# Splitting GpSimd's elementwise operations into two halves in a fused attention and expert kernel

## The chip, the cores and the metric

The kernel runs on one core of one Trainium2 chip. The metric is the device time of one execution in microseconds, given as the median of several runs. The times before are 1339.83, 1334.39 and 1337.75 us, median 1337.75.

A core has five engines that work side by side, each with an instruction queue of its own: TensorE (PE in the profile; PEld is its weight load), VectorE (DVE), ScalarE (ACT), GpSimd (POOL) and SyncE (SP, here the issuer of almost all transfers). They wait for each other by semaphores.

## The reference

```python
q_lm, k_lm = segment_mean(q), segment_mean(k)      # 576 rows to 32 landmarks
A, Bm, C = sm(q, k_lm), sm(q_lm, k_lm), sm(q_lm, k)
Z = Bm.T / (norm1(Bm) * norminf(Bm) + 1e-6)
for _ in range(6):
    Z = 2 * Z - Z @ Bm @ Z
x = A @ Z @ C @ v                                  # 8 batches, 8 heads, 576 x 64
x = relu(x @ w_in) ** 2 @ w_out                    # 4608 x 512, hidden 2048
e = argmax(x @ w_gate)                             # one of 8 experts for a token
out = gate(x, e) * sigmoid(x @ w_output_gate)[e] * (relu(x @ w1[e]) @ w2[e])   # hidden 1024
```

`sm` is a scaled softmax of a matrix product; everything is float32.

## The kernel before, in words

The work goes by batch (8 of 576 tokens). Three kinds of work share the core:

- **Attention of a batch** (`unit`): sums of segments (`sums`, line 382), scores, three softmaxes, the iterated inverse (`inverse`), all small. `softmax_a` (lines 463 to 478) takes the 128 x 576 scores `aa`: VectorE's maximum (468), GpSimd's subtraction (469), ScalarE's exponential (472), VectorE's sum and reciprocal (474 to 476), GpSimd's product (477), VectorE's transpose (671). Attention's product with the first weight is folded into a matrix `g` for a batch, made from `win` (`g_alone`, `g_steps`).
- **The first feed-forward network of a batch** (`gemm`, `second`): two column halves `c` of 288 tokens, and in each 16 blocks `f` of 128 hidden units. A block is 6 matmuls (line 998), ReLU on ScalarE (1009), two squares (1011 on VectorE or 1013 on ScalarE, and 1014), the low part `gl` on VectorE (1015), then 12 matmuls into four accumulators (1048).
- **The experts** (`experts`): batch by batch, 8 blocks of 128 hidden units, 24 matmuls (line 1238) and 14 more (1274, 1286) a block.

Products are made in a reduced format with two parts for each operand: `split` (line 186) lets ScalarE round a tile to a high part (188), and then GpSimd, or VectorE where `lo_eng` says so, subtracts it from the raw tile to give the low part (191). TensorE then multiplies high by high, high by low and low by high. The low parts on GpSimd are those of `gb` (from `gr`), `ab` (from `ar`), `wi`, three of four `wo`, the activations `xs` (128 x 1152) and the first weights `s` of the experts (128 x 512); the second weights' go to VectorE.

Weights of the first network pass through `convert` (lines 137 to 184), which rebuilds a 32-bit float from two integer words: ScalarE makes `m` and `r` (153, 154), VectorE shifts and joins bits (163, 164), GpSimd adds the two as integers (167). Two kinds of job use it: `w_in`, whose result goes to memory as `win`, and `w_out`, whose result is split into `wo`.

Around 40 to 130 us the conversions and the attention of the first batches run together with the first blocks of `gemm`. Up to about 700 us the attention of later batches runs as side work beside `gemm`: at each `point` a share of a side step (RATES, RATE) is put into the program. From about 700 to 910 us `gemm` runs almost alone; from there on it is the experts. `behind` and `follow` add ordering edges that pace TensorE and ScalarE. The program is laid out by a planner that orders each engine's queue by priority and a timed model of the program (it is told `schedule_with_timeline_sim=True`); within a queue the order is then fixed. SyncE's queue issues the transfers: `win`, `g`, `at`, `x2`, the experts' weights. GpSimd issues 9 small ones.

The expert weights are prepared one block ahead of their use:

```python
            fetch_w(i + 2)
            flush()
            h = hidden(i)
            parts_w(i + 1)
```

Of the kernel before, what the change touches and what calls it, by code (L numbers as in the profile page):

```python
# [9 lines left out]
F32 = mybir.dt.float32  # L10
F32R = mybir.dt.float32r
I32 = mybir.dt.int32
U32 = mybir.dt.uint32
ACTF = mybir.ActivationFunctionType
ALU = mybir.AluOpType
# [68 lines left out]
class Kernel:  # L84
# [42 lines left out]
    def convert(self, jobs):  # L127

        nc, pool = self.nc, self.cv
        W = CONV_W
        pieces = [(j, c) for j in range(len(jobs)) for c in range(0, 512, W)]
        st, to = {}, {}  # L140
        RB = CONV_AHEAD

        def fetch(i):
            j, c = pieces[i]
            raw = pool.tile([128, W, 2], I32, tag="raw", name="raw", bufs=RB)
            nc.sync.dma_start(out=raw, in_=jobs[j][0][:, c:c + W].bitcast(I32).rearrange("p (n t) -> p n t", t=2))
            st[i] = raw

        def scale(i):
            raw = st[i]  # L150
            m = pool.tile([128, W], I32, tag="cm", name="m", bufs=CONV_BUFS)
            r = pool.tile([128, W], I32, tag="cr", name="r", bufs=CONV_BUFS)
            first = nc.scalar.activation(out=m.bitcast(F32), in_=raw[:, :, 1].bitcast(F32), func=ACTF.Abs, scale=2.0 ** -111)
            nc.scalar.activation(out=r, in_=raw[:, :, 0].bitcast(U32), func=ACTF.Copy, scale=2.0 ** -29)
            if self.last_gb is not None:
                self.follow(first, self.last_gb)
            st[i] = raw, m, r

        def bits(i):
            (j, c), (raw, m, r) = pieces[i], st.pop(i)  # L160
            if c == 0:
                to[j] = jobs[j][1]()
            nc.vector.tensor_scalar(out=m, in0=m, scalar1=3, scalar2=None, op0=ALU.logical_shift_left)
            nc.vector.scalar_tensor_tensor(  # L164
                out=m, in0=raw[:, :, 1], scalar=-0x80000000, in1=m, op0=ALU.bitwise_and, op1=ALU.bitwise_or
            )
            nc.gpsimd.tensor_tensor(out=to[j][:, c:c + W].bitcast(I32), in0=m, in1=r, op=ALU.add)

        n = len(pieces)
        for i in range(min(RB - 1, n)):  # L170
            fetch(i)
        yield STEP
        per = 512 // W
        for i in range(n + 4):
            if i + RB - 1 < n:
                fetch(i + RB - 1)
            if i < n:
                scale(i)
            if 0 <= i - 1 < n:
                bits(i - 1)  # L180
            if i >= 2 and (i - 2) % per == per - 1 and i - 2 < n:
                j = (i - 2) // per
                jobs[j][2](to.pop(j))
            yield STEP

    def split(self, t, raw, lo_eng=None, late=False):

        hi = self.nc.scalar.copy(out=t[:, 0], in_=raw)  # L188
        if late and self.last_h is not None:
            self.follow(hi, self.last_h)  # L190
        (lo_eng or self.nc.gpsimd).tensor_tensor(out=t[:, 1], in0=raw, in1=t[:, 0].bitcast(F32), op=ALU.subtract)  # L191

    def convert_in(self):

# [268 lines left out]
    def softmax_a(self, u, hg):  # L463
        nc = self.nc
        ma = u["ma"][:, :, hg]
        af = u["aa"][:, hg].rearrange("p (n l) -> p n l", l=LM)
        wide = [128, NB, LM]
        nc.vector.tensor_reduce(out=ma[:, 0], in_=af, axis=AX.X, op=ALU.max)
        (nc.vector if u["early"] else nc.gpsimd).tensor_tensor(
            out=af, in0=af, in1=ma[:, 0].unsqueeze(2).to_broadcast(wide), op=ALU.subtract  # L470
        )
        nc.scalar.activation(out=af, in_=af, func=ACTF.Exp, scale=SCALE / SEG)
        yield STEP
        nc.vector.tensor_reduce(out=ma[:, 1], in_=af, axis=AX.X, op=ALU.add)
        nc.vector.tensor_scalar(out=ma[:, 1], in0=ma[:, 1], scalar1=1e-9, scalar2=None, op0=ALU.add)
        nc.vector.reciprocal(out=ma[:, 2], in_=ma[:, 1])
        nc.gpsimd.tensor_tensor(out=af, in0=af, in1=ma[:, 2].unsqueeze(2).to_broadcast(wide), op=ALU.mult)
        yield STEP

    def scores_c(self, u, hg, c):  # L480
# [1017 lines left out]
```

## Time and profile before

| | |
|---|---|
| median of 3 runs | 1337.75 us (1334.39 to 1339.83) |
| profiled execution | 1340.34 us, span 1338.5 us |
| TensorE busy | 1275.7 us, 95% |
| VectorE busy | 781.5 us, 58% |
| ScalarE busy | 633.6 us, 47% |
| GpSimd busy | 384.5 us, 29%, 311 instructions |
| mean granted TensorE clock | 0.977 of full speed |

The span is the time from the first to the last instruction on the chip. Busy time of GpSimd and VectorE counts an instruction from its start in the record to its end; when it starts and can't go on, the wait is inside. Busy shares are means over stages with different limits. The chain that ended last is followed back from the last instruction, at each step to what released it; it tells whose time set the end.

### The profile page before, as it was taken

The page shows a single profiled execution, that of the slowest core. Times are in us where ns is not written, and L with a number is a line of the kernel's source. Part 1 is how long each engine was busy: PE and PEld are TensorE (multiplying, and loading weights), DVE is VectorE, ACT ScalarE, POOL GpSimd, SP SyncE. Part 2 cuts the span into 40 slices and gives each one's busy share as a digit, 9 for nine tenths or more (in the row PEclk, how much of TensorE's full clock was granted, in tenths as well). Part 3 has the DMA queues.
Part 4 walks back from the last instruction along what each step waited for, and adds up shares of the span by engine and source line. Part 5 has one row for each costly group of instructions (what it writes and reads, how often), then busy time and mean ns, then how long its engine had stood idle before and what let it go on. Part 6 is the DMA issues. An engine that isn't in the chain of part 4 may idle for free.

```text
span 1338.5 us, 25101 instructions
## 1 busy us (share of the span) xinstructions
PE 1275.7 (95%) x9458; PEld 1114.2 (83%) x9458; DVE 781.5 (58%) x1743; ACT 633.6 (47%) x1402; POOL 384.5 (29%) x311
## 2 busy tenths in 40 slices
PE   6587999999999999999999999999999999999997
PEld 4276868688788888898989999998888888888886
DVE  7999868768769897687653433454423233233231
ACT  5596454445535557545654344344334334334331
POOL 3566112113013034313622112024323323233120
PEclk7588999999999999999999999999999999999999
DMA  9866283462623247613652112014344354342321
GB/s 324 273 222 192 86 269 85 173 199 89 217 70 112 72 127 211 172 63 95 206 146 67 43 35 67 1 48 146 99 130 139 100 156 120 109 150 92 116 93 38
DMA packets 126587, 172.38 MB, mean 129 GB/s; under 512 B 10558, under 2 KB 84062, under 8 KB 126462
## 3 DMA queue, kind: packets, MB, share of 16 engines
q1 hardware_dynamic: 126030, 170.11, 41.6%
q8 instruction: 76, 1.25, 0.4%
q0 software_dynamic: 288, 0.43, 0.1%
q14 instruction: 49, 0.40, 0.1%
q10 hardware_dynamic: 144, 0.20, 0.0%
HBM read 128.19 MB, written 42.51 MB: 128 GB/s over the span
## 4 chain that ended last, share of the span: by engine, by line
PE 74%; DVE 11%; DMA 7%; ACT 3%; issue 2%; POOL 1%; SPq 1%; POOLq 0%; DVEq 0%; ACTq 0%
PE acc L1048 24%; PE hp L1238 15%; PE y L1274 13%; PE hp L998 11%; PE bank L346 6%; PE y L1286 2%; DMA raw<-in_moe_w_in_dram 2%; DVE sums L382 2%; DVE gl L1015 2%; DMA g<-gs 2%; DVE g L1011 1%; PE pl L1075 1%; DVE m L164 1%; DMA w<-win 1%; DMA t<-in_q_dram 1%
## 5 line engine op out<-in xcount | busy, mean ns | idle before, releaser
L1048 PE MATMUL acc<-gh,wo 128*128 128x288 f32 x2048 | 459.2, 300 | 1.6 <-POOL wo L191 0.7
L1048 PEld LDWEIGHTS acc<-gh,wo 128*128 128x128 f32 x2048 | 344.1, 190 | 27.1 <-issue 18.2
L1048 PE MATMUL acc<-gl,wo 128*128 128x288 f32 x1024 | 290.3, 301 | 10.2 <-DVE gl L1015 9.7
L998 PE MATMUL hp<-ab,gb 128*128 128x288 f32 x1536 | 254.8, 301 | 0.9 <-ACT r L1009 0.5
L998 PEld LDWEIGHTS hp<-ab,gb 128*128 128x128 f32 x1536 | 217.7, 189 | 19.6 <-issue 6.9
L1011 DVE TENSOR_TENSOR g<-r 128x288 f32<-128x288 f32 x239 | 130.3, 546 | 162.5 <-ACT r L1009 161.7
L1009 ACT ACTIVATE r<-hp 128x288 f32<-128x288 f32 x256 | 105.8, 413 | 245.1 <-PE hp L998 240.6
L1238 PEld LDWEIGHTS hp<-xs,s 128*128 128x128 f32 x1536 | 210.7, 188 | 9.0 <-issue 0.9
L1238 PE MATMUL hp<-xs,s 128*128 128x288 f32 x1536 | 215.5, 295 | 0.0
L1048 PEld LDWEIGHTS acc<-gl,wo 128*128 128x128 f32 x1024 | 194.6, 190 | 22.8 <-DVE gl L1015 17.5
L1274 PE MATMUL y<-s,h 128*128 128x512 f32 x768 | 190.3, 395 | 0.0
L1274 PEld LDWEIGHTS y<-s,h 128*128 128x128 f32 x768 | 141.0, 188 | 29.4
L1015 DVE TENSOR_TENSOR gl<-g,gh 128x288 fp32r<-128x288 f32 x256 | 143.2, 560 | 26.8 <-ACT gh L1014 8.9
L191 POOL TENSOR_TENSOR s<-r,s 128x512 fp32r<-128x512 f32 x64 | 83.1, 1299 | 245.6 <-ACT s L188 245.6
L191 DVE TENSOR_TENSOR s<-r,s 128x512 fp32r<-128x512 f32 x64 | 53.1, 830 | 154.4 <-ACT s L188 154.4
L191 POOL TENSOR_TENSOR gb<-gr,gb 128x512 fp32r<-128x512 f32 x56 | 74.5, 1331 | 226.6 <-ACT gb L188 143.6
L188 ACT CAST s<-r 128x512 fp32r<-128x512 f32 x128 | 78.2, 616 | 118.8 <-PE y L1286 92.6
L1247 DVE SCALAR_TENSOR_TENSOR h<-hp,h 128x64 fp32r<-128x64 f32 (+2 forms) x192 | 62.6, 354 | 109.5 <-ACT h L1244 109.5
L1014 ACT ACTIVATE gh<-r 128x288 fp32r<-128x288 f32 x256 | 114.4, 447 | 6.4
L1244 ACT ACTIVATE h<-hp 128x288 fp32r<-128x288 f32 x128 | 52.6, 411 | 132.1 <-PE hp L1238 118.2
L382 DVE TENSOR_REDUCE sums<-t 128x32 f32<-128x576 f32 x64 | 71.2, 1165 | 9.3 <-DMA t<-in_q_dram 5.8
L191 POOL TENSOR_TENSOR xs<-xr,xs 128x1152 fp32r<-128x1152 f32 x16 | 45.7, 2860 | 68.3 <-ACT xs L188 63.2
(195 smaller groups left out, 1350.8 us busy)
## 6 DMA issues: line engine op xcount, KB each, us to landing
r<-in_moe_w_dram SPq DMA_DIRECT2D x128, 256.0 KB
w<-win SPq DMA_DIRECT2D x80, 256.0 KB
gr<-g SPq DMA_DIRECT2D x56, 256.0 KB
t<-in_k_dram SPq DMA_DIRECT2D x16, 576.0 KB
t<-in_q_dram SPq DMA_DIRECT2D x16, 576.0 KB
v<-in_v_dram SPq DMA_DIRECT2D x48, 192.0 KB
x_d<-x SPq DMA_DIRECT2D x16, 576.0 KB
xr<-x_d SPq DMA_DIRECT2D x16, 576.0 KB
```

Of the source, the lines that this page charges most:

```text
L188: hi = self.nc.scalar.copy(out=t[:, 0], in_=raw)
L191: (lo_eng or self.nc.gpsimd).tensor_tensor(out=t[:, 1], in0=raw, in1=t[:, 0].bitcast(F32), op=ALU.subtract)
L346: self.last_pe = self.nc.tensor.matmul(out, **kw)
L382: self.nc.vector.tensor_reduce(out=s[:, 0, ds], in_=t[:, :, ds].rearrange("p s d -> p d s"), axis=AX.X, op=ALU.add)
L998: mm = nc.tensor.matmul(hp[:, 0:HC], lhsT=g[:, l, hg, fs], rhs=at[:, r, hg, :], start=(i == 0), stop=(i == 5))
L1009: nc.scalar.activation(out=r, in_=hp[:, 0:HC], func=ACTF.Relu, scale=1.0 / 256)
L1011: nc.vector.tensor_tensor(out=g2, in0=r, in1=r, op=ALU.mult)
L1014: nc.scalar.activation(out=gh, in_=r, func=ACTF.Square)
L1015: nc.vector.tensor_tensor(out=gl, in0=g2, in1=gh.bitcast(F32), op=ALU.subtract)
L1048: nc.tensor.matmul(acc[m][:, 0:HC], lhsT=self.wo[f][:, l, ms], rhs=r, start=(f == 0 and i == 0), stop=(f == NFC - 1 and i == 2),)
L1238: nc.tensor.matmul(hp[:, 0:HC], lhsT=s1[:, l, kk, :], rhs=xs[j, c][:, r, kk, :], start=(k == 0), stop=(k == 3 * KD - 1),)
L1274: mm = nc.tensor.matmul(acc[t], lhsT=l, rhs=s2[:, r, :], start=(first and k == 0), stop=(last and k == 2))
```

## The change

Every elementwise operation of GpSimd on data is issued as two instructions of half the columns each: the integer add of `convert`, the low parts of `split` and the two of `softmax_a`. For operands with three axes the halves are taken along the second axis. Operations of VectorE stay whole, and so does GpSimd's copy of the sums (line 385).

```diff
@@ convert
-            nc.gpsimd.tensor_tensor(out=to[j][:, c:c + W].bitcast(I32), in0=m, in1=r, op=ALU.add)
+            self.halves(to[j][:, c:c + W].bitcast(I32), m, r, ALU.add)
@@ split
-        (lo_eng or self.nc.gpsimd).tensor_tensor(out=t[:, 1], in0=raw, in1=t[:, 0].bitcast(F32), op=ALU.subtract)
+        if lo_eng is None:
+            self.halves(t[:, 1], raw, t[:, 0].bitcast(F32), ALU.subtract)
+        else:
+            lo_eng.tensor_tensor(out=t[:, 1], in0=raw, in1=t[:, 0].bitcast(F32), op=ALU.subtract)
+
+    def halves(self, out, in0, in1, op):
+
+        n = out.shape[1]
+        for p in (slice(0, n // 2), slice(n // 2, n)):
+            self.nc.gpsimd.tensor_tensor(out=out[:, p], in0=in0[:, p], in1=in1[:, p], op=op)
@@ softmax_a
-        (nc.vector if u["early"] else nc.gpsimd).tensor_tensor(
-            out=af, in0=af, in1=ma[:, 0].unsqueeze(2).to_broadcast(wide), op=ALU.subtract
-        )
+        most = ma[:, 0].unsqueeze(2).to_broadcast(wide)
+        if u["early"]:
+            nc.vector.tensor_tensor(out=af, in0=af, in1=most, op=ALU.subtract)
+        else:
+            self.halves(af, af, most, ALU.subtract)
...
-        nc.gpsimd.tensor_tensor(out=af, in0=af, in1=ma[:, 2].unsqueeze(2).to_broadcast(wide), op=ALU.mult)
+        self.halves(af, af, ma[:, 2].unsqueeze(2).to_broadcast(wide), ALU.mult)
```

## Rows read from the trace of the kernel before

**Rows 1.** The page: busy time of the engines, and the chain's shares by engine.
```profile
PE 1275.7 (95%) x9458; PEld 1114.2 (83%) x9458; DVE 781.5 (58%) x1743; ACT 633.6 (47%) x1402; POOL 384.5 (29%) x311
...
PE 74%; DVE 11%; DMA 7%; ACT 3%; issue 2%; POOL 1%; SPq 1%; POOLq 0%; DVEq 0%; ACTq 0%
```

**Rows 2.** Busy us by stretch: PE, PEld, DVE, ACT, POOL; clock, DMA share, GB/s.
```profile
40.00:130.00 90.00, 66.59 (x542) 49.70 (x541) 86.78 (x140) 67.77 (x158) 57.80 (x44) 0.81 0.71 223
...
400.00:550.00 150.00, 143.97 (x1263) 127.99 (x1257) 125.36 (x258) 86.60 (x201) 50.74 (x45) 1.00 0.46 140
...
910.00:1339.00 429.00, 418.79 (x2473) 372.23 (x2471) 136.32 (x311) 153.48 (x294) 122.52 (x83) 0.99 0.39 114
```

**Rows 3.** Groups by shape of POOL, count; busy, mean ns; idle before, releaser.
```profile
L191 POOL TENSOR_TENSOR s<-r,s 128x512 fp32r<-128x512 f32 x64 | 83.1, 1299 | 245.6 <-ACT s L188 245.6
...
L191 POOL TENSOR_TENSOR ab<-at,ab 128x576 fp32r<-128x576 f32 x1 | 1.6, 1603 | 0.0
```

**Rows 4.** Timeline of DVE: start us, duration us, what, idle before.
```profile
75.17 0.69 DVE L164 SCALAR_TENSOR_TENSOR m<-raw,m 128x512 int32<-128x512 int32 x1
...
76.52 1.07 DVE L163 TENSOR_SCALAR m<-m 128x512 int32<-128x512 int32 x1 [0.33 <-ACT m L153]
77.63 1.66 DVE L164 SCALAR_TENSOR_TENSOR m<-raw,m 128x512 int32<-128x512 int32 x1
...
740.49 0.46 DVE L1011 TENSOR_TENSOR g<-r 128x288 f32<-128x288 f32 x1 [1.31 <-ACT r L1009]
...
890.74 2.20 DVE L1011 TENSOR_TENSOR g<-r 128x288 f32<-128x288 f32 x1 [1.30 <-ACT r L1009]
893.07 0.46 DVE L1015 TENSOR_TENSOR gl<-g,gh 128x288 fp32r<-128x288 f32 x1
```

**Rows 5.** Groups by shape of DVE.
```profile
L1015 DVE TENSOR_TENSOR gl<-g,gh 128x288 fp32r<-128x288 f32 x256 | 143.2, 560 | 26.8 <-ACT gh L1014 8.9 <-DVE g L1011 0.5 <-DVE bc L587 0.3
L1011 DVE TENSOR_TENSOR g<-r 128x288 f32<-128x288 f32 x239 | 130.3, 546 | 162.5 <-ACT r L1009 161.7
...
L164 DVE SCALAR_TENSOR_TENSOR m<-raw,m 128x512 int32<-128x512 int32 x32 | 32.3, 1010 | 0.6
```

**Rows 6.** Timeline of POOL.
```profile
76.03 1.28 POOL L167 TENSOR_TENSOR w<-m,r 128x512 int32<-128x512 int32 x1 [1.78 <-DVE m L164]
77.27 1.47 POOL L191 TENSOR_TENSOR wo<-w,wo 128x512 fp32r<-128x512 f32 x1
...
889.95 2.67 POOL L191 TENSOR_TENSOR xs<-xr,xs 128x1152 fp32r<-128x1152 f32 x1 [32.31 <-ACT xs L188]
897.74 2.67 POOL L191 TENSOR_TENSOR xs<-xr,xs 128x1152 fp32r<-128x1152 f32 x1 [5.12 <-ACT xs L188]
```

**Rows 7.** The chain in order of time: start us, us, what (some of its pieces).
```profile
49.12 1.50 DVE m L164
...
84.41 1.34 POOL w L167
...
129.04 0.93 DVE dg L647
...
357.48 1.35 DVE gl L1015
...
646.57 1.19 DVE ma L475
...
662.79 1.31 POOL wi L191
...
1009.58 3.17 PE hp L1238 x24
...
1016.02 3.19 PE hp L1238 x24
```

**Rows 8.** PE alone by stretch: us, busy us (instructions), clock, DMA share, GB/s.
```profile
640.00:660.00 20.00, 19.58 (x141) 1.00 0.65 192
...
720.00:740.00 20.00, 20.00 (x154) 1.00 0.23 71
```

## Prediction

> **What bounds the kernel now.** I first read the page's busy shares and the shares of the chain that ended last. TensorE is busy 95% of the span and carries 74% of the chain; VectorE carries 11% and GpSimd 1%, at 29% busy [rows 1]. An engine with so much room can be made less efficient without harm, unless its work stands in someone's way. So the second view is the busy time by stage [rows 2]. From 40 to 130 us VectorE is busy 86.8 of 90 us and TensorE only 66.6: VectorE is the bound there. From 400 to 550 us both are nearly full (125 and 144 of 150). From 910 us to the end TensorE has 418.8 of 429 us and GpSimd's 122.5 us lie wholly beside it.
>
> The third view is the list of instruction groups. The change splits eleven GpSimd groups, from 64 low parts of `s` to the one of `ab` [rows 3]: 258 instructions in all.
>
> The fourth is the timeline, and it shows what GpSimd does to VectorE. Undisturbed, lines 1011 and 1015 take 0.46 us each and line 164 takes 0.69 [rows 4]; their means over the run are 0.546, 0.560 and 1.010 us [rows 5]. The excess is 239 x 0.086 + 256 x 0.10 + 32 x 0.32 = 56 us. Where it comes from is seen at 77.63 us: line 164 lasts 1.66 us [rows 4] while a GpSimd subtraction runs from 77.27 to 78.74 [rows 6]; 78.74 plus the line's own 0.6 is its end, 79.29. VectorE waited until the whole GpSimd instruction was over. At 890.74 us line 1011 lasts 2.20 us beside a GpSimd instruction that runs from 889.95 to 892.62 [rows 4, 6]: the same.
>
> The last view is the chain in order of time: which of these waits set the end. From 40 to 130 us it holds 15 VectorE pieces of 0.87 us or more that are at most 0.69 undisturbed, the first at 49.12, the last at 129.04 [rows 7]: 20.0 us less 6.8 undisturbed, 13.2 us of waiting. From 330 to 700 us there are 12 such, 357.48 to 646.57 [rows 7], 15.9 less 4.2, so 11.7 us. Near 900 us there are two, the first at 890.74 [rows 4], of 1.75 us excess each. That is 28 us of waiting on the chain. GpSimd's own elementwise instructions on it are 13, from 84.41 to 662.79 [rows 7].
>
> **The change part by part.** *Two instructions for one.* Alone, 512 columns take 1.28 us and 1152 take 2.67 [rows 6]: 2.17 ns a column and 0.17 us beside. A half of 512 columns is thus 0.73 us, a pair 1.45 less the 0.04 us by which back-to-back records overlap (76.03 + 1.28 against 77.27) [rows 6]: +0.13 us a pair, 258 x 0.13 = 33 us more of GpSimd. It has 950 us free, and in the last stage each low part is made one step ahead, 6.4 us (1016.02 less 1009.58) [rows 7]: hidden there at 0. If that lead were gone, the 64 low parts of `s` would cost 8 us. On the chain it is 13 x 0.13 = 1.7, say +1.5 us. The wait of ScalarE or VectorE on a low part moves to the second half; that is this same 0.13 us, with nothing else queued behind.
>
> *Halves let VectorE in sooner.* No row shows a split operation, so I bound it. At best each wait on the chain halves: 13.2 to 6.6, 11.7 to 5.9, 3.5 to 1.8, a gain of 14 us. At worst nothing is gained. What decides is the instruction behind the one that waited. At 76.52 us line 163 waits, runs, and line 164 behind it waits again, for the next GpSimd instruction [rows 4, 6]: the two engines take turns. With halves, VectorE's first gets in after 0.73 us, GpSimd's second half then goes, and VectorE's second waits for that. If both VectorE instructions need their turn, the later ends as before. At 890.74: the first half would end at about 891.36, line 1011 at 891.8, the second half at 893.2, line 1015 at 893.65; today that ends at 893.53 [rows 4]. Gain 0, so I take **0 for the third term**. From 40 to 130 us lines 163, 164, 191 and 1015 follow each other closely with VectorE 96% busy, nearest to this case: **-1.5 us** of 0 to -6.6. From 330 to 700 us I count five waiting pieces of line 1015, which often has a transpose or a reduction behind it, five of line 1011, with 1015 following, and two others. Half of the former's 4.5 us is gained, and a tenth of the other 7.2: **-3 us** of 0 to -5.9.
>
> Whether VectorE gets a turn between two halves is the open step. The rows at 76.52 and 77.27 show that line 163 got in between two back-to-back GpSimd instructions: the wait ended as the first ended (77.31), and the second lasted 1.47 rather than 1.28 us [rows 4, 6]. I take it so. The Trainium skill, GPSIMD Engine Reference, section Instruction dispatch, speaks against it: completion of a Pool instruction "does not hold back the next Pool instruction", a core begins the next as soon as its share is done. By that rule the halves would run as one, the gains would be zero and the sum +1.5 us or a little more; no row here shows a pair with nothing at all between.
>
> *Sum:* -1.5 - 3 + 0 + 1.5 = -3 us. The profiled execution took 1340.3 us, 2.6 above the median of 1337.75. So 1337.3 by that execution and **1335 us** by the median: no difference of note, since a measurement of this kernel can tell about 0.5% (6.7 us). When the waits shrink, the next late thing is TensorE's own queue (144 of 150 us busy from 400 us on).
>
> **The rivals.** *Full relief (faster).* Non-waiting VectorE work fills the turns, all waits halve, and the lost time downstream (gl late, matmuls late) returns too: -14 + 1.5, so about 1325. For it: VectorE near its limit in both stretches. Against: the turns at 76.52 and 890.74.
>
> *The halves are not parted (no change).* The port stays taken through both: waits as before, each 0.13 us longer; 29 waits x 0.13 + 1.5 is +5: 1343. The row at 77.27 speaks against it [rows 6]. The section of the Trainium skill named above leads here.
>
> *Late pairs (slower).* Place: the run of GpSimd work on the chain from 636 to 664 us (seven of the 13) and at 309 to 316 (three). Now GpSimd too waits at two starts: VectorE's 0.45 to 0.69 us twice, so a pair can reach 1.41 + 0.55 to 0.69, 2.0 to 2.1 us, in place of 1.3. Price: 13 x 0.75 = 10 us with no relief: 1348. It decides where the mean pair, first start to last end, passes 1.28 + 0.55 = 1.83 us (13 x 0.55 = 7 us) while lines 1011 and 1015 don't fall below their present means. For it: GpSimd instructions follow each other on the chain around 640 us. Against: GpSimd has 1% of the chain in all [rows 1].
>
> *Another order.* The queues' order comes from a planner that times the program; 258 more instructions may reorder all engines. No row shows how its order depends on such lengths. One more disturbed stretch costs little: TensorE starts 141 instructions in 640 to 660 us against 154 in 720 to 740 [rows 8], 13 x 0.13 = 1.7 us in 20. Four to five such would pass 0.5%; it can go either way, 1327 to 1345.
>
> **How the numbers follow.** The forecast has 0.40 (its own range 1330 to 1341); full relief 0.22; unparted halves 0.10; late pairs 0.13; another order 0.15. Faster by over 0.5%: all of full relief, 0.05 of the forecast, 0.06 of another order: 0.33. Slower: all of late pairs, 0.05 of unparted halves, 0.06 of another order and 0.02 of the forecast: 0.26. Same is the rest, 0.41. The range runs from below full relief, 1321, to the late pairs' 1348.
>
> **What would show it.** Right: means of lines 1011 and 1015 near 0.50 us, line 164 near 0.85; pairs of 512 columns at 1.4 to 1.6 us; 569 GpSimd instructions; the stage from 910 us on unchanged in length; the stretch of 40 to 130 us shorter by under 5 us. Wrong: line 1015 unchanged (unparted halves); a pair mean over 1.83 us with more GpSimd on the chain (late pairs); 400 to 550 us shorter by over 5 us (full relief); other neighbours in the queues with a moved stage (another order).

## The result and the profile after

The changed kernel takes 1325.18 us (median; 1323.49 to 1326.16) against 1337.93 before: ratio 0.9903, 95% interval [0.9887, 0.9919], so 12.8 us or 1.0% faster. The forecast was 1335 us.

The page of the changed kernel, busy times and the chain, against [rows 1]:

```profile
PE 1270.4 (96%) x9458; PEld 1110.4 (84%) x9458; DVE 751.2 (57%) x1743; ACT 634.2 (48%) x1402; POOL 439.7 (33%) x569
...
PE 80%; DVE 9%; DMA 4%; ACT 3%; issue 2%; POOL 1%; SPq 0%; POOLq 0%; ACTq 0%; DVEq 0%
```

GpSimd does 258 instructions more and is busy 55 us longer; VectorE, whose instructions are the same 1743, is busy 30 us less. Lines 1011 and 1015 are now 1022 and 1026; helper line 200 issues all halves. Groups by shape of VectorE, against [rows 5], then two of GpSimd:

```profile
L1022 DVE TENSOR_TENSOR g<-r 128x288 f32<-128x288 f32 x239 | 120.5, 505 | 167.8 <-ACT r L1020 166.8
...
L1026 DVE TENSOR_TENSOR gl<-g,gh 128x288 fp32r<-128x288 f32 x256 | 135.7, 531 | 25.7 <-ACT gh L1025 7.9 <-DVE g L1022 0.5
...
L164 DVE SCALAR_TENSOR_TENSOR m<-raw,m 128x512 int32<-128x512 int32 x32 | 28.1, 879 | 0.7
```

```profile
L200 POOL TENSOR_TENSOR s<-r,s 128x256 fp32r<-128x256 f32 x128 | 97.4, 782 | 233.5 <-ACT s L188 233.5
```

The excess of the three VectorE groups over their undisturbed times falls from 56 us to 239 x 0.045 + 256 x 0.071 + 32 x 0.19 = 35 us. A pair of `s` has 97.4 / 64 = 1.52 us of busy time, where one whole operation had 1.30 [rows 3].

The stretches, against [rows 2]:

```profile
40.00:130.00 90.00, 70.97 (x583) 54.16 (x580) 81.91 (x146) 70.34 (x164) 71.39 (x87) 0.82 0.71 230
400.00:550.00 150.00, 147.80 (x1312) 131.85 (x1311) 120.83 (x270) 87.87 (x201) 61.68 (x84) 1.00 0.50 149
```

In the same 150 us TensorE starts 1312 matmuls in place of 1263, and VectorE, with 12 instructions more (270 against 258), is busy 4.5 us less.

How one wait changed is seen in the timeline of GpSimd (first fence) and VectorE (second) at the place that was 890 us before [rows 4, 6]:

```profile
874.03 3.02 POOL L200 TENSOR_TENSOR xs<-xr,xs 128x576 fp32r<-128x576 f32 x2 [32.17 <-ACT xs L188]
```

```profile
874.81 0.95 DVE L1022 TENSOR_TENSOR g<-r 128x288 f32<-128x288 f32 x1 [1.30 <-ACT r L1020]
875.90 1.47 DVE L1026 TENSOR_TENSOR gl<-g,gh 128x288 fp32r<-128x288 f32 x1
```

Line 1022 got in between the halves: it lasts 0.95 us in place of 2.20. GpSimd's pair took 3.02 us instead of 2.67; 0.13 us of that is the estimate for a second start, the rest is the wait of its second half. Then line 1026 waited for that half. From the start of line 1022 to the end of line 1026 it is 2.56 us, and was 2.79: two waiters, hardly any gain. The Trainium skill, GPSIMD Engine Reference, section Instruction dispatch, says that the completion of a GpSimd instruction does not hold back the next one; the row shows that VectorE is let in between two halves all the same.

The order of the queues changed as well, on every engine: the planner placed the program anew. VectorE's sequence of conversions, blocks and attention is another one from its 100th instruction on, which starts at 44.29 us. So two things happened at once, and the first experiments part them.

### The profile page after: what moved, and what is told of

Its sections match the earlier page's. It is cut to its first block, busy times and chain, and to the rows that moved or that the text cites. A ratio compares the mean times of both kernels' runs of the same rounds, so it can differ in the third digit from the quotient of the medians.

```text
span 1321.8 us, 25393 instructions
## 1 busy us (share of the span) xinstructions
PE 1270.4 (96%) x9458; PEld 1110.4 (84%) x9458; DVE 751.2 (57%) x1743; ACT 634.2 (48%) x1402; POOL 439.7 (33%) x569
## 4 chain that ended last, share of the span: by engine, by line
PE 80%; DVE 9%; DMA 4%; ACT 3%; issue 2%; POOL 1%; SPq 0%; POOLq 0%; ACTq 0%; DVEq 0%
PE acc L1059 26%; PE hp L1249 15%; PE y L1285 13%; PE hp L1009 13%; PE bank L355 7%; PE y L1297 2%; DVE sums L391 2%; DMA gr<-g 2%; PE pl L1086 1%; DVE gl L1026 1%; DMA g<-gs 1%; DVE m L164 1%; DVE x L422 1%; PE bank L358 1%; PE pt L1112 1%
## 5 line engine op out<-in xcount | busy, mean ns | idle before, releaser
L1022 DVE TENSOR_TENSOR g<-r 128x288 f32<-128x288 f32 x239 | 120.5, 505 | 167.8 <-ACT r L1020 166.8
L200 POOL TENSOR_TENSOR s<-r,s 128x256 fp32r<-128x256 f32 x128 | 97.4, 782 | 233.5 <-ACT s L188 233.5
L200 POOL TENSOR_TENSOR gb<-gr,gb 128x256 fp32r<-128x256 f32 x112 | 84.4, 774 | 213.7 <-ACT gb L188 141.0
L1026 DVE TENSOR_TENSOR gl<-g,gh 128x288 fp32r<-128x288 f32 x256 | 135.7, 531 | 25.7 <-ACT gh L1025 7.9
L194 DVE TENSOR_TENSOR s<-r,s 128x512 fp32r<-128x512 f32 x64 | 47.0, 734 | 158.6 <-ACT s L188 158.6
L200 POOL TENSOR_TENSOR xs<-xr,xs 128x576 fp32r<-128x576 f32 x32 | 46.2, 1467 | 65.7 <-ACT xs L188 60.7
```

What stands on the lines that cost most here:

```text
L200: self.nc.gpsimd.tensor_tensor(out=out[:, p], in0=in0[:, p], in1=in1[:, p], op=op)
L1022: nc.vector.tensor_tensor(out=g2, in0=r, in1=r, op=ALU.mult)
L1026: nc.vector.tensor_tensor(out=gl, in0=g2, in1=gh.bitcast(F32), op=ALU.subtract)
```

## The experiments

A time is the median of its runs; ratios are to the kernel before on the same chip. Where it says *cut after planning*, the program is planned first, and the instruction lists of the finished plan are then edited: the order of all other queues stays as it was. The first half takes the waits of the whole operation, the second signals its end. The core of the edit:

```python
for k in range(parts):
    done.append(i.__replace__(
        ins=tuple(_cut(x, k, parts) for x in i.ins),
        outs=tuple(_cut(x, k, parts) for x in i.outs),
        sync_info=SyncInfo(on_wait=sync.on_wait if k == 0 else [],
                           on_update=sync.on_update if k == parts - 1 else [])))
```

### Is it the halves or the order?

**Halves in the order of before** (e1):

```diff
     with _tile.TileContext(nc, schedule_with_timeline_sim=True) as tc:
         nystrom_moe_kernel(tc, *args)
+    _split_planned(nc, 2, None)
```

> The program is planned as before, so that every queue has the order of before; only then is each of the 258 GpSimd operations cut into two halves where it stands. The change gained 12.8 us, and its planned order differs from that of before on all engines. Theory A (the waits of VectorE on GpSimd's port are shorter): this kernel keeps most of the gain, 1325 to 1330 us, and the means of lines 1011 and 1015 fall from 0.546 and 0.560 us to about 0.50 and 0.53 us, as in the changed kernel. Theory B (the planner's new order made the gain): 1335 to 1341 us, whatever the means do.

**Whole operations in the order of after** (e2): the changed kernel is planned, then neighbouring halves are joined.

```diff
+    _merge_planned(nc)
```

> The program is planned as after the change, so that every queue has the order of after; then each pair of halves that stands side by side on GpSimd's queue is made one whole operation again (all but one pair). Theory A (shorter waits on the port): the gain is lost, 1334 to 1341 us, means of lines 1022 and 1026 (1011 and 1015 of before) back at 0.54 to 0.56 us. Theory B (the new order): 1323 to 1328 us. Between them, 1328 to 1334 us: both have a share.

One pair of `gb` did not stand side by side and stays in halves, so e2 has 312 GpSimd instructions.

| | whole | halves |
|---|---|---|
| order of before | 1337.24 | 1330.98, ratio 0.9959 [0.9946, 0.9973] |
| order of after | 1340.13, ratio 1.0024 [1.0013, 1.0036] | 1325.18, ratio 0.9903 [0.9887, 0.9919] |

The halves gain in either order: 6.3 us in that of before and 15.0 in that of after. (The last cell was timed in another session than the other three; by the ratios, each to the kernel before on the same chip, the halves gain 0.41% and 1.21%.) The new order alone loses 2.9 us. So theory B is out: the order by itself gained nothing in all. But theory A isn't all either: e1 lies 1 us above its range, and with halves the new order is 5.8 us the better one. The groups of VectorE in e1 (first fence) and e2 (second):

```profile
L1015 DVE TENSOR_TENSOR gl<-g,gh 128x288 fp32r<-128x288 f32 x256 | 135.4, 530 | 27.1 <-ACT gh L1014 9.1 <-DVE g L1011 0.5 <-DVE bc L587 0.3
L1011 DVE TENSOR_TENSOR g<-r 128x288 f32<-128x288 f32 x239 | 122.3, 513 | 169.6 <-ACT r L1009 168.9
```

```profile
L1026 DVE TENSOR_TENSOR gl<-g,gh 128x288 fp32r<-128x288 f32 x256 | 150.1, 587 | 23.5 <-ACT gh L1025 5.6 <-DVE g L1022 0.5
L1022 DVE TENSOR_TENSOR g<-r 128x288 f32<-128x288 f32 x239 | 133.1, 558 | 158.8 <-ACT r L1020 157.9
```

In the order of after whole operations meet VectorE harder than they did before (0.587 and 0.558 us against 0.560 and 0.546); halves meet it about as much in both orders. That fits the loss of the whole operations. It doesn't explain why halves are faster in the new order, as their means are the same in both.

Where the order counts, the profiles show by stretches. A column half of the first network ends with the evacuation of its accumulators, the copies of the sums into `x`. The table has the start of the last evacuation on VectorE (line 1056, after the change 1067) in the first column half, the time from there to that of the 11th, and the length of the 16th, the last:

| us | first ends at | from there to the 11th | the last |
|---|---|---|---|
| whole, order of before | 141.8 | 562.0 | 46.0 |
| halves, order of before (e1) | 135.8 | 558.7 | 45.5 |
| whole, order of after (e2) | 147.5 | 552.9 | 49.2 |
| halves, order of after | 138.8 | 549.1 | 45.5 |

The first and the 11th in e2, then in the changed kernel, and the 11th before and in e1 (their first are shown further down):

```profile
147.47 0.45 DVE L1067 TENSOR_SCALAR x<-acc 128x288 f32<-128x288 f32 x1
700.41 0.45 DVE L1067 TENSOR_SCALAR x<-acc 128x288 f32<-128x288 f32 x1
```

```profile
138.77 0.45 DVE L1067 TENSOR_SCALAR x<-acc 128x288 f32<-128x288 f32 x1
687.88 0.45 DVE L1067 TENSOR_SCALAR x<-acc 128x288 f32<-128x288 f32 x1
```

```profile
703.81 0.45 DVE L1056 TENSOR_SCALAR x<-acc 128x288 f32<-128x288 f32 x1
```

```profile
694.46 0.45 DVE L1056 TENSOR_SCALAR x<-acc 128x288 f32<-128x288 f32 x1
```

In the middle stretch the new order is 9 to 10 us shorter, with whole operations as with halves. Whole operations give that back at both ends: 5.7 us in the first column half and 3.2 in the last, where halves give back 3.0 us and nothing. So the order does gain by itself, in one stretch, and halves keep it from losing as much in the others. These are single profiles, and two of one program differ by up to 4 us in the middle stretch (553.3 in e8, 549.1 in e12, both described below); but e10, in the order of before, has 562.1, and two more runs of halves in the order of after (e5, e11) have 548.1 and 549.5. What the new order does better there is not shown.

### Is it the shorter hold, or the second start?

**As many instructions but one, cut into 17 parts and 1 part in 18** (e10), in the order of before; of the 258 operations the one that makes `ab` from `at` stays whole:

```diff
-    a, b = n * k // of, n * (k + 1) // of
+    a, b = (0, n - n // 18) if k == 0 else (n - n // 18, n)
```

> The order of before, each operation cut after planning into two instructions as in the first experiment, but of 17 and 1 parts in 18 of the columns (484 and 28 of 512): as many instructions, as much fixed cost, but the long one blocks the port nearly as long as the whole. Theory A (what helps is that one instruction holds the port for half as long): no relief, 1337 to 1342 us, means of lines 1011 and 1015 at 0.54 to 0.57 us. Rival (any second start lets VectorE in, or the number of instructions does something else): 1329 to 1334 us.

1336.62 us, ratio 0.9993 [0.9976, 1.0011]. The groups of VectorE:

```profile
L1015 DVE TENSOR_TENSOR gl<-g,gh 128x288 fp32r<-128x288 f32 x256 | 146.6, 573 | 24.9 <-ACT gh L1014 7.0 <-DVE g L1011 0.5 <-DVE bc L587 0.3
L1011 DVE TENSOR_TENSOR g<-r 128x288 f32<-128x288 f32 x239 | 127.4, 534 | 164.5 <-ACT r L1009 163.5
L164 DVE SCALAR_TENSOR_TENSOR m<-raw,m 128x512 int32<-128x512 int32 x32 | 26.4, 824 | 0.6
```

This is just below the range of theory A, and with as many starts as in e1 the gain of e1 is missing: a second start by itself, with its cost, changes nothing that can be measured. What helps is that one instruction holds VectorE up for half as long. (Line 164 did get shorter, 0.824 us, and one profile can't say why; the time didn't follow.) The run doesn't price the fixed cost alone: its interval, from -3.2 to +1.5 us, is for the cost together with whatever relief this cut gives.

### Is it what the first half releases early?

In the changed kernel many first halves signal their own end, so a reader of those columns, or the next user of a buffer, may go on sooner; in e1 none does. **The signal moved to the second half** (e5; the edit in words, not in code):

```diff
-    first half: on_update=[own signal]     second half: on_update=[own signal]
+    first half: on_update=[]               second half: on_update=[both signals]
```

> The changed kernel, planned as it is, but where the first half of a pair signals its end by itself, the signal is moved to the second half, so that nobody can go on after the first half alone. The halves still part on the port. Theory A (VectorE's shorter waits are all): 1324 to 1327 us, no difference to the changed kernel. Rival (part of the gain comes from readers and from freed buffers that need only the first half, which the halves cut after planning in the order of before could not have): 1327 to 1333 us.

1325.58 us, ratio 0.9905 [0.9888, 0.9921]: the same as the changed kernel within the noise. Early release is worth nothing here that can be measured, and it isn't what e1 lacked.

### Where do the halves pay?

The changed kernel in its own order, with one group of pairs joined again after planning. The group's names are the argument:

```diff
+    _merge_planned(nc, ("wf", "w", "wo"))          # e6: conversions
+    _merge_planned(nc, ("gb", "ab", "aa", "wi"))   # e7: beside the first network
+    _merge_planned(nc, ("s1", "xs"))               # e8 and e12: experts
```

> The changed kernel in its planned order, but the pairs of the conversions and of the low parts of wo (40 to 130 us) are whole again. The prediction's step for this stretch gave halves a relief of 1.5 us there: 1325 to 1328 us. Rival: with whole operations everywhere the same order ended its first column half of the first network at 147 us in place of 139; if that is the share of this stretch and is kept, 1331 to 1335 us.

> The changed kernel in its planned order, but the pairs of gb, ab, aa and wi (the work beside the first network) are whole again. The prediction's step gave a relief of 3 us there, less 1 us of fixed cost: 1326 to 1329 us. Rival: all of the loss of whole operations in this order (15 us) that the first 140 us do not hold, some 7 us: 1330 to 1334 us.

> The changed kernel in its planned order, but the pairs of the experts' low parts (s and xs) are whole again. The prediction costed both the fixed cost and the relief there at nothing, as TensorE is the bound: 1324 to 1326.5 us. Rival: the waits of lines 1022 and 1026 on the first xs operations near 875 and 882 us cost something that the halves had saved, or a low part that comes earlier frees TensorE: 1327 to 1330 us.

| whole again | us | ratio to before | loss against 0.9903 |
|---|---|---|---|
| conversions (e6) | 1330.15 | 0.9937 [0.9921, 0.9953] | 0.0034, 4.5 us |
| beside the first network (e7) | 1330.49 | 0.9932 [0.9913, 0.9951] | 0.0029, 3.9 us |
| experts (e8) | 1330.60 | 0.9935 [0.9915, 0.9954] | 0.0032, 4.3 us |

Each stage holds about as much; together 12.7 us of the 16 that joining all of them costs (1.0024 less 0.9903). Each loss has an uncertainty of some 2 us or more, by the intervals. The conversions' loss lies between the two ranges expected, that beside the first network in the rival's, that of the experts just above the rival's. The experts' share was unexpected, and e8's profile was odd: it had lost 5 us between 140 and 264 us, ahead of anything that it edits. So it was **run again beside the changed kernel** (e11, e12):

> The changed kernel once more, beside the next one on the same chip: 1323 to 1327 us.

> The kernel with whole operations in the experts once more. Its profile had lost 5 us between 140 and 264 us, in waits for transfers, before the first instruction that it changes. If that was chance of the transfers: within 2 us of the changed kernel beside it. If the program as such is slower: again 4 to 6 us above it.

The changed kernel again: 1324.18 us, 0.9904 [0.9876, 0.9932]. With whole experts' operations: 1327.82 us, 0.9932 [0.9909, 0.9954], 3.6 us more: between the two outcomes expected, but the slowest run of the changed kernel, 1326.11 us, is still faster than the fastest of the other, 1327.08. The odd stretch did not come again: between the ends of the first and the third column half e8 took 125.1 us, e12 120.9 and the changed kernel 120.4. So it was chance, and the loss is not. Whether transfers made it isn't shown. Where the loss lies, the timelines show: e12 first (VectorE, then GpSimd), then VectorE of e11.

```profile
892.66 3.08 DVE L194 TENSOR_TENSOR s<-r,s 128x512 fp32r<-128x512 f32 x2 [0.53 <-ACT s L188]
895.66 2.95 DVE L1022 TENSOR_TENSOR g<-r 128x288 f32<-128x288 f32 x1
898.53 0.51 DVE L1258 SCALAR_TENSOR_TENSOR h<-hp,h 128x224 fp32r<-128x224 f32 x2
898.96 2.46 DVE L1026 TENSOR_TENSOR gl<-g,gh 128x288 fp32r<-128x288 f32 x1
```

```profile
895.42 5.68 POOL L200 TENSOR_TENSOR xs<-xr,xs 128x1152 fp32r<-128x1152 f32 x2 [0.24 <-ACT xs L188]
```

```profile
892.34 0.99 DVE L1022 TENSOR_TENSOR g<-r 128x288 f32<-128x288 f32 x1
...
894.59 1.06 DVE L1026 TENSOR_TENSOR gl<-g,gh 128x288 fp32r<-128x288 f32 x1 [0.82 <-ACT gh L1025]
```

Two operations of 1152 columns follow each other while the last blocks of the first network still need lines 1022 and 1026. Whole, they make VectorE wait 2.5 and 2.0 us (the rows less 0.46), and TensorE with it: the last column half ends 49.5 us after the one ahead of it, against 45.6 with halves (e12 and e11). That is 3.9 us of the 6.1 by which the two profiles differ; 1.6 us are there before it and 0.7 come after. So most of the loss lies at these few operations. From the last `gemm` block on, the experts' stage takes about as long as ever: from the first to the last low part of `h` 411.6 us in the kernel before, 411.4 in the changed one.

### Would smaller parts be better, or another order?

**Quarters**, in the order of before (e3) and by cutting the changed kernel's halves (e4); softmax operations go into three parts, or six:

```diff
-    _split_planned(nc, 2, None)
+    _split_planned(nc, 4, None)
```

> The order of before, each GpSimd operation cut into four where it stands (the softmax ones into three). GpSimd's busy time grows by some 0.13 us for each cut more, 258 x 3 x 0.13 = 100 us over before. Theory A: the waits get shorter again, lines 1011 and 1015 at 0.47 to 0.52 us, and the time is that of the halves in the same order or up to 6 us below. Turn-taking rival: between two operations of VectorE the next quarter goes, so nothing more is gained, or late quarters cost 2 to 10 us over the halves. Theory B: as before the change, 1335 to 1345 us.

> The order of after, each half cut into two again where it stands. Theory A: 1318 to 1326 us. If late pairs on GpSimd or the fixed cost of an instruction weigh more than the shorter waits: 1327 to 1335 us. Theory B: 1324 to 1328 us, no difference to the changed kernel.

1345.08 us, 1.0068 [1.0048, 1.0089], and 1338.91 us, 1.0010 [0.9997, 1.0024]: 14 us above the halves in either order, above every range expected, and in the first case slower than before the change. The lines wait less (0.502 and 0.504 us), so the relief is there. The chain's shares by engine and the stretch from 40 to 130 us of e3 tell what took its place:

```profile
PE 72%; POOL 6%; DMA 5%; DVE 4%; issue 2%; ACT 2%; SPq 1%; POOLq 0%; ACTq 0%; DVEq 0%
```

```profile
40.00:130.00 90.00, 67.54 (x541) 51.87 (x542) 68.43 (x137) 66.76 (x156) 84.56 (x157) 0.81 0.69 224
```

GpSimd is now the bound of that stretch, with 84.6 of 90 us, and VectorE has room (68.4; 86.8 before [rows 2]). GpSimd's fixed costs and its turns behind VectorE have moved onto the chain: 6%, from 1%. (This chain can be followed back only to 105 us, so its shares add up to 92%.) That stretch is half of the loss: the first column half of e3 ends at 141.8 us, 6.0 us later than in e1, and from there to the 11th it takes 565.5 us, 6.8 us longer. There GpSimd is far from full, 211 of 565 us busy, but its pieces of the chain add up to 43 us, against 24 in e1 and 14 before.

**The conversions planned whole, then cut** (e9). In profiles, the order of before with halves had reached the end of the first column half at 135.8 us, that of after at 138.8; this run tries to have both.

```diff
-            self.halves(to[j][:, c:c + W].bitcast(I32), m, r, ALU.add)
+            nc.gpsimd.tensor_tensor(out=to[j][:, c:c + W].bitcast(I32), in0=m, in1=r, op=ALU.add)
...
+    _split_planned(nc, 2, lambda i: i.outs[0].memref.split("_")[0] in ("wf", "w", "wo"))
```

> All operations in halves, but the conversions and the low parts of wo are planned as whole operations and cut after planning. With halves, the order of before reached the end of the first column half at 135.8 us, the order of after at 138.8, and the order of after was faster in all that follows (764 us to the end of the last column half against 771). If the order of the first stretch can be had without giving up that of the rest: 1320 to 1324 us. If the planner's order changes throughout: 1324 to 1332 us.

1329.83 us, 0.9946 [0.9929, 0.9963]. The plan changed throughout: a third order, with halves everywhere. So halves give 1331.0, 1329.8 and 1324 to 1325 us in three orders; none of the variants tried is faster than the changed kernel.

## Why the prediction was wrong in size

Its direction of cause held: VectorE waits less on GpSimd, in the changed kernel GpSimd still has 1% of the chain, and the experts' stage itself doesn't move. The size was -12.8 us in place of -3. The measured 1325.18 us lies outside the 1330 to 1341 that the forecast gave as its own, inside the whole range of 1321 to 1348. It meets the 1325 of the rival *full relief* by luck: the halves alone gave 1331 (e1), with some 36 us of the three groups' excess of 56 left, and so not halved, and the order gave the rest. By its steps:

- **The first term, -1.5 us for 40 to 130 us, was mis-sized.** In the order of before (e1) the first column half ends 6.0 us sooner, and joining the conversions' pairs again costs 4.5 us (e6): nearly the upper bound of 6.6. The medians of e6 are the firmer figure, three times the forecast. The 6.0 us are from one profile each, and the mean granted TensorE clock from 40 to 130 us was 0.88 of full speed in e1 and 0.81 before; the changed kernel, at 0.82, is 3.0 us sooner, and e10, which gains nothing in all, 3.2. The last accumulator evacuation of that column half in the kernel before and in e1:

```profile
141.79 0.45 DVE L1056 TENSOR_SCALAR x<-acc 128x288 f32<-128x288 f32 x1
```

```profile
135.75 0.45 DVE L1056 TENSOR_SCALAR x<-acc 128x288 f32<-128x288 f32 x1
```

  The step held that turns give back what the first waiter gains. That is right for two waiters and a single GpSimd operation. But here GpSimd has the next one ready, and each VectorE instruction waits for one GpSimd instruction whatever comes next: a half rather than a whole. This is read from rows and not tested by a run of its own. The timelines of the changed kernel, VectorE and then GpSimd:

```profile
86.14 0.95 DVE L163 TENSOR_SCALAR m<-m 128x512 int32<-128x512 int32 x1
87.12 1.10 DVE L164 SCALAR_TENSOR_TENSOR m<-raw,m 128x512 int32<-128x512 int32 x1
```

```profile
83.83 2.06 POOL L200 TENSOR_TENSOR wo<-w,wo 128x256 fp32r<-128x256 f32 x2
85.98 1.70 POOL L200 TENSOR_TENSOR w<-m,r 128x256 int32<-128x256 int32 x2
```

  Lines 163 and 164 each wait about 0.5 us, behind the first and the second half of the pair that begins at 85.98; at 77.63 line 164 alone waited 1.0 [rows 4]. The backlog passes to GpSimd (a pair takes 1.7 to 2.1 us), which had the time.
- **The second term, -3 us for 330 to 700 us, held** in the order of before: from the end of the first column half to 703.81 (before) and 694.46 (e1) it is 562.0 and 558.7 us, 3.3 us less. The same program's profiles differ by up to 4 us in such stretches, and the stretches of e1 add up to more than its gain: the two profiled executions are 9.9 us apart by their spans, the medians 6.3. So this is agreement, not proof. In the order of after, joining these pairs costs 3.9 us (e7).
- **The third term, 0, held:** the last column half takes 46.0 us before, 45.5 in e1 and 45.5 in the changed kernel, and, as shown above, it held in its very rows. The 3.6 us that whole operations cost in the order of after (e12) are no gain over the kernel before, where the last column half shows 0.5 us for them.
- **The fixed cost, +1.5 us,** is priced by no run alone; the interval of e10 leaves it open. A pair of `s` is busy 0.22 us longer than a whole, not 0.13; part of that can be its second half's wait for VectorE. The longer work isn't hidden in every order: in e1 GpSimd has 4% of the chain, in the kernel before and in the changed one 1%.

```profile
PE 75%; DVE 10%; DMA 5%; POOL 4%; issue 2%; ACT 2%; SPq 1%; POOLq 0%; DVEq 0%; ACTq 0%
```

- **Unparted halves** is refuted by the row at 874.81. **Late pairs** came true with quarters: with GpSimd busy 94% of a stretch, e3 is slower than before. With halves the mean pair of `s`, 1.52 us, stays under the 1.83 us that it needed.
- **Another order** was set beside the forecast as an alternative and put at nothing in the sum. In fact it came on top: about half of the 12.8 us, but as a net gain only together with halves. It lies in the stretch from the first column half to the 11th, 9 to 10 us shorter in the profiles. What in the planner makes it so was not tried; e5 excludes that it is the early signals.

By parts: halves in the old order -6.3 us, the order that was planned with them another -5.8, by medians of different sessions, which add up to 12.1; by the ratios 0.41% and 0.56%, of 0.97% in all.

## What to carry to other kernels

When two engines block each other for the length of a whole instruction, cut the instruction of the engine that has time: what counts is how long a single one holds the other up, not how busy either is. Stop before the cut engine's own work, longer by its fixed costs and turns, comes onto the chain, in a stretch that it fills or one in which it is late; here halves gain 1% and quarters lose it all. And where a planner sets the order, price the edit with the old order and the new one apart: the same order cost 0.2% with whole operations and gained 0.4 to 0.6% with halves.

## What was not expected of the hardware

The two engines take turns at the finest grain tried. In e3 lines 1011 and 1015 both get in while four quarters of `xs` run (VectorE first, then GpSimd), but over the run their means fall only to 0.504 and 0.502 us, not to the undisturbed 0.46:

```profile
894.23 1.11 DVE L1011 TENSOR_TENSOR g<-r 128x288 f32<-128x288 f32 x1 [1.30 <-ACT r L1009]
895.47 0.85 DVE L1015 TENSOR_TENSOR gl<-g,gh 128x288 fp32r<-128x288 f32 x1
```

```profile
893.45 3.55 POOL L191 TENSOR_TENSOR xs<-xr,xs 128x288 fp32r<-128x288 f32 x4 [31.64 <-ACT xs L188]
```

And what a further GpSimd instruction costs depends on where it stands: 257 uneven second parts cost no time that can be measured, while 486 to 576 more instructions than the halves cost 14 us, half of it where GpSimd became nearly full, in a stretch of 90 us in which it had 58 us of work before [rows 2].
